# The weights' block sums made by adding DMA transfers: links set further apart, chains of different blocks between, and the third layer's sums moved to the second sweep

## The chip, the cores and the metric

One core of one Trainium2 chip runs the whole program. The metric is device microseconds (us) of that core for one execution.

## What is computed

The inputs are float32 and hold attention (4 batches, 12 heads, 448 tokens, 64 per head) and two pairs of feed-forward layers on the 1792 tokens (448 per batch, 768 wide). Cut to what matters:

```
q_n, k_n = rmsnorm(q, g_q), rmsnorm(k, g_k)
attn = softmax(q_n @ k_n.T / sqrt(64)) @ v
x = attn with heads side by side            # 1792 x 768
x = (sigmoid(x @ w_gate) * (x @ w_val)) @ w_out       # 768 -> 1536 -> 768
r = max(x @ w_in, 0); out = (r * r) @ w_out2          # 768 -> 2048 -> 768
```

## The kernel before, in words

The weights are worked through as 68 blocks of 128x768 numbers. Every product of a layer is made of three TensorE passes (high part by high part, high by low, low by high), so each block is split by ScalarE (`wsp<-wraw`, line 193, high part) and VectorE (line 194, low part) just before it is used. `w_load` (line 149) fetches a block on SyncE's DMA queue (SP) into one of three `wraw` buffers, and `w_ahead` keeps the loads and the splits a few blocks ahead of the use.

The program has four stages. A prologue does the attention of batch 0. `sweep(0)` takes batch 0 through all layers while the attention of batch 1 runs between its products; it also writes each converted block to DRAM (`w32`, line 182, on GpSimd's queue, POOL). `sweep(1)` takes batch 1 through all layers, in 204 steps, while the attention of batches 2 and 3 (twelve pairs of heads, some 16 or 17 steps each) runs between. Last, `joint` takes batches 2 and 3 through the layers together.

`joint` saves TensorE work by a scheme with seven products where eight blocks would be multiplied (`seven`). For it some operands are sums and differences of blocks of the weights. These are made in DRAM by DMA alone, and each such sum is two transfers of 192 KB: a copy on SP (line 596) and then an adding transfer on POOL (line 598, `accum_op=ALU.add`). A chain belongs to one pair of blocks and has three links, with two sums in the first and one in each of the others; a link reads what the link before it left in DRAM, so its copy waits until the adding transfer before has landed, and its adding transfer until its copy has landed. There are 12 chains for the first layer (`ws`, from `pair_chains`), 8 for the third (`wu`) and 8 for the last (`wt`, from `quad_chains`): 48, 32 and 32 sums.

Before, `add_up` issues all copies of a link on SP and at once all its adding transfers on POOL. `steps_of_1` puts the three links of chain p of the first layer at steps 12p+5, 12p+9 and 12p+13 of the second sweep. The third layer's chains are issued one link after the other in `joint`'s first layer (two links after each `seven`), and the last layer's in `joint`'s second layer (w_out, two links at each block) and after it.

Both queues run in order. SP also issues the weights' loads, the loads of q, k and v, and two transfers of the attention which move halves of `qs` and `ks` to other partitions (`a_dma`, lines 434 and 430); the scores of the next pair of heads (`att<-ks,qs`) wait for these. POOL also computes the power -0.5 of the rms norm (`ms<-ms,mhalf`, line 261), which VectorE needs for scaling q and k (line 265), which TensorE then transposes (`acc<-ident,qk`, line 571), and it spreads the softmax's reciprocals (`sb<-su`, line 320). In the second sweep and in `joint` TensorE's order is that of the program; the order on the other engines comes from a scheduler, which keeps every sum's transfers behind the last product issued before them (`held`), without a wait on the chip.

Of the kernel before, what the change touches and what calls it, by code (L numbers as in the profile page):

```python
# [12 lines left out]
ALU = mybir.AluOpType  # L13
# [4 lines left out]
def attention_moe_moe2_kernel(  # L18
# [541 lines left out]
    def held(i):  # L560
        tc.add_manual_dep(
            i.ins, latest[0].ins.name,
            mybir.DependencyInfo(mybir.DependencyClass.NoSync, mybir.DependencyReason.SCHED_ONLY), reason="order")
# [11 lines left out]
    def mm3(o, wb, kk, xh, xl, start, stop):  # L575
        wh, wl = wb[:, 0, kk], wb[:, 1, kk]
        mm(out=o, lhsT=wh, rhs=xh, start=start, stop=False)
        mm(out=o, lhsT=wh, rhs=xl, start=False, stop=False)
        mm(out=o, lhsT=wl, rhs=xh, start=False, stop=stop)
# [11 lines left out]
            halves.extend((wb[:, :, 0:3], wb[:, :, 3:6]))  # L591
        return halves.pop(0)

    def add_up(sums):
        for dst, first, second in sums:
            held(nc.sync.dma_start(out=dst, in_=first))
        for dst, first, second in sums:
            held(nc.gpsimd.dma_start(out=dst, in_=second, accum_op=ALU.add))  # L598

    def pair_chains(i0, i1, t):  # L600
        a11, a12, a21, a22 = (w32[i][:, h:h + 384] for i in (i0, i1) for h in (0, 384))
        s = [t[:, 384 * n:384 * (n + 1)] for n in range(4)]
        return [[(s[0], a21, a22), (s[2], a11, a21)], [(s[1], s[0], a11)], [(s[3], s[1], a12)]]
# [47 lines left out]
    def seven(parts):  # L651
        a, a2, b = (acc_tile()[:, :N] for _ in range(3))
        ps = att_tile()
        c, d = ps[:, 0, :N], ps[:, 1, :N]

        def product(o, name, start=True, stop=True):
            w = operand()
            for kk in range(3):
                mm3(o, w, kk, *parts[name, kk], start and kk == 0, stop and kk == 2)

        base = tmp("base")
        product(a, "B11")
        nc.scalar.copy(out=base, in_=a)
        product(a2, "B21")
        product(c, "T1")
        c11 = tmp("c11")
        nc.vector.tensor_tensor(out=c11, in0=a2, in1=base, op=ALU.add)
        yield 0, 0, c11, 1
        product(b, "T2")
        nc.vector.tensor_tensor(out=base, in0=base, in1=b, op=ALU.subtract)  # L670
        product(d, "T3")
        u = one.tile([128, 2, N], F32, tag="vs", name="u")
        nc.vector.tensor_tensor(
            out=u, in0=ps[:, :, :N], in1=base.unsqueeze(1).to_broadcast([128, 2, N]), op=ALU.add)
        c22 = tmp("c22")
        nc.vector.tensor_tensor(out=c22, in0=c, in1=u[:, 1], op=ALU.add)  # L676
        yield 1, 1, c22, -1
        last = att_tile()
        product(last[:, 1, :N], "T4")
        product(last[:, 0, :N], "B22")  # L680
        nc.vector.tensor_tensor(out=u, in0=last[:, :, :N], in1=u, op=ALU.add)
        yield 0, 1, u[:, 0], 1
        yield 1, 0, u[:, 1], -1

    def joint():
        edge = att_tile()
        for kc in range(NF + 1):
            n = 128 if kc < NF else TAIL
            nc.tensor.transpose(edge[:n, 0, kc * QR:(kc + 1) * QR], ident[:QR, :n], ident[:QR, :QR])
        later_sums = [c for kb in range(K4) for c in quad_chains(kb)]  # L690
        third_sums = [c for m in range(K2 // 2) for c in pair_chains(W3 + 2 * m, W3 + 2 * m + 1, w3s[m])]
        hr = one.tile([128, 27, N], F32R, tag="hr", name="h")
        rt = one.tile([128, 9, N], F32R, tag="rt", name="h")
        room = [hr[:, i] for i in range(27)] + [rt[:, i] for i in range(9)]
# [1 line left out]
        for g in range(K1 // 2):  # L696
            if g == 3:
                xy = one.tile([128, 12, N], F32R, tag="xy0", name="h")
                room += [xy[:, i] for i in range(12)]
            s = {}  # L700
            for i in range(2):
                q = two.tile([128, 2, N], F32, tag="qk", name="s")
                for n in range(2):
                    s[i, n] = q[:, n]
            for m, n, t, sign in seven(xp):
                e = s[m, n]
                nc.scalar.activation(out=e, in_=t, func=AF.Relu, scale=-1.0 * sign)
                nc.scalar.activation(out=t, in_=t, func=AF.Abs)
                nc.scalar.activation(out=e, in_=e, func=AF.Exp, scale=-1.0)
                nc.scalar.activation(out=t, in_=t, func=AF.Tanh, scale=0.5)  # L710
                nc.vector.scalar_tensor_tensor(out=e, in0=t, scalar=1.0, in1=e, op0=ALU.add, op1=ALU.mult)
            for c in (third_sums.pop(0) for _ in range(min(2, len(third_sums)))):
                add_up(c)
            for m, n, o, sign in seven(xp):
                e = s[m, n]
                if sign > 0:
                    nc.vector.tensor_tensor(out=e, in0=o, in1=e, op=ALU.mult)
                else:
                    nc.vector.scalar_tensor_tensor(
                        out=e, in0=o, scalar=-1.0, in1=e, op0=ALU.mult, op1=ALU.mult)  # L720
                hi, lo = room.pop(0), room.pop(0)
                h[2 * g + m, n] = hi, lo
                nc.scalar.copy(out=hi, in_=e)
                nc.vector.tensor_tensor(out=lo, in0=e, in1=hi.bitcast(F32), op=ALU.subtract)
            for c in (third_sums.pop(0) for _ in range(min(2, len(third_sums)))):
                add_up(c)
        order.extend(["raw64"] * 3 + ["qs", "xy1", "pt", "kq", "kq", "p", "p", "p"])
        yp = {}
        for j2 in range(3):
            y = {}  # L730
            for r in range(2):
                j = j2 + 3 * r
                q = two.tile([128, 2, N], F32, tag="qk", name="y")
                o = [acc_tile()[:, :N] for _ in range(2)]
                for b2 in range(2):
                    wb = block()
                    if later_sums or third_sums:
                        for _ in range(2):
                            if third_sums:
                                add_up(third_sums.pop(0))  # L740
                            elif later_sums:
                                add_up(later_sums.pop(0))
                    for kk in range(6):
                        k1 = 6 * b2 + kk
                        for n in range(2):
                            mm3(o[n], wb, kk, *h[k1, n], k1 == 0, k1 == K1 - 1)
                for n in range(2):
                    y[r, n] = q[:, n]
                    nc.scalar.activation(out=y[r, n], in_=o[n], func=AF.Copy, scale=0.5)
                split(yp, "B11" if r == 0 else "B21", j2, y[r, 0])  # L750
            split(yp, "B22", j2, y[1, 1])
            sums_of(yp, j2, y[0, 0], y[0, 1], y[1, 0], y[1, 1])
# [8 lines left out]
        for m2 in range(K2 // 2):  # L761
            for m, n, o, sign in seven(yp):
                k = 2 * m2 + m
                dst = r_of(k)[:, n * N:(n + 1) * N]
                nc.vector.scalar_tensor_tensor(
                    out=dst, in0=o, scalar=0.0, in1=o, op0=ALU.max if sign > 0 else ALU.min, op1=ALU.mult)
                if n == 1:
                    src = r_of(k)[:, 768:896]
                    nc.scalar.copy(out=plain[:, k, 0], in_=src)
                    nc.vector.tensor_tensor(  # L770
                        out=plain[:, k, 1], in0=src, in1=plain[:, k, 0].bitcast(F32), op=ALU.subtract)
            for _ in range(2):
                if later_sums:
                    add_up(later_sums.pop(0))
        for c in later_sums:
            add_up(c)
        yield
        row0 = 2 * N
        fsum = [rest[:, 768 * i:768 * (i + 1)].rearrange("p (k n) -> p k n", k=2) for i in range(3)] + [
# [508 lines left out]
    next(pro, None)  # L1288
    def steps_of_1():
        at = {}  # L1290
        for p in range(K1):
            for n, c in enumerate(pair_chains(4 * (p // 2) + p % 2, 4 * (p // 2) + 2 + p % 2, w1s[p])):
                at.setdefault(12 * p + 4 * n + 5, []).append((add_up, (c,)))
        order.extend(["xy1", "raw64", "raw64", "raw64", "kq", "qs", "kq", "p", "p", "pt", "p"])
        for j in range(3):
            for i, what in enumerate(("B11", "B21")):
                at.setdefault(158 + 6 * j + 3 * i, []).append((x_part, (j, what)))
        for i, what in enumerate(("sums", "B22")):
            at.setdefault(180 + 4 * i, []).append((x_part, (0, what)))
            at.setdefault(195 + 3 * i, []).append((x_part, (1, what)))  # L1300
        return at
# [63 lines left out]
```

## Time and profile before

| | us |
|---|---|
| median of 3 runs (1281.50, 1281.73, 1286.24) | 1281.73 |
| the profiled execution | 1287.66 |
| its span, first to last instruction | 1285.9 |
| TensorE busy in the span | 1243.1 (97%) |
| VectorE, ScalarE, GpSimd busy | 948.3, 792.0, 229.6 |
| chain of waits: TensorE 70%, DMA 15% of the span | |

The span is what the trace covers; the execution's own time has 1.8 us more around it. TensorE's busy time counts matmuls that run at a lower clock as busy too, so time is lost in idle pieces and in stretches with a lower granted clock.

### The profile page before, as it was taken

What the parts mean: (1) busy time and instruction counts of PE and PEld (TensorE: products, weight loads), DVE (VectorE), ACT (ScalarE), POOL (GpSimd) and SP (SyncE); (2) the same over time, 40 slices, a digit from 0 to 9 for tenths busy, and PEclk for the clock granted to TensorE, in tenths of its full rate; (3) what the DMA queues carried; (4) which work ended last, traced back from release to release, by engine and by line L of the source; (5) the groups of instructions that cost most, each with busy time, mean ns of one, the idle gap of its engine ahead of it and who ended that gap; (6) DMA issues with size and microseconds to landing.
All of it is one profiled execution on the core that took longest, in us unless ns stands there. A gap on an engine that the chain in (4) does not pass through costs nothing.

```text
span 1285.9 us, 19138 instructions
## 1 busy us (share of the span) xinstructions
PE 1243.1 (97%) x6599; PEld 1084.8 (84%) x6599; DVE 948.3 (74%) x1492; ACT 792.0 (62%) x1603; POOL 229.6 (18%) x236
## 2 busy tenths in 40 slices
PE   9999999999999989999999899999999996999998
PEld 6545788878879988888888899999999985999998
DVE  5866997878974878887878867888874324889873
ACT  5766887767865868776788765756672322235451
POOL 3311223212210322222222110011112221000000
PEclk8999999999999989999999999999999997999999
DMA  5445998888786776778777332577778777333443
GB/s 142 97 129 156 313 338 271 272 270 266 242 300 187 175 160 163 168 169 194 155 167 174 87 90 82 142 186 182 198 186 179 160 154 166 111 111 99 134 130 117
DMA packets 200545, 225.81 MB, mean 176 GB/s; under 512 B 83968, under 2 KB 178176, under 8 KB 200448
## 3 DMA queue, kind: packets, MB, share of 16 engines
q1 hardware_dynamic: 177024, 175.36, 47.0%
q0 software_dynamic: 21568, 48.77, 17.9%
q8 instruction: 52, 0.85, 0.3%
q10 hardware_dynamic: 1856, 0.46, 0.2%
q14 instruction: 45, 0.37, 0.1%
HBM read 185.99 MB, written 76.28 MB: 204 GB/s over the span
## 4 chain that ended last, share of the span: by engine, by line
PE 70%; DMA 15%; DVE 5%; ACT 4%; issue 3%; POOL 2%; SPq 1%; POOLq 0%; DVEq 0%; ACTq 0%
PE acc L566 41%; PE att L566 15%; DMA wt<-w 5%; DMA ws<-w 3%; PE att L291 3%; DMA ws<-ws 2%; PE att L571 2%; DMA wt<-wt 2%; POOL ms L261 2%; PE acc L345 2%; PE att L345 1%; PE acc L912 1%; PE acc L327 1%; DMA ks<-ks 1%; PE att L327 1%
## 5 line engine op out<-in xcount | busy, mean ns | idle before, releaser
L194 DVE TENSOR_TENSOR wsp<-wraw,wsp 128x768 fp32r<-128x768 f32 x246 | 236.4, 962 | 117.5 <-ACT wsp L193 115.4
L193 ACT CAST wsp<-wraw 128x768 fp32r<-128x768 f32 x246 | 205.6, 836 | 189.0 <-PE att L566 62.3
L566 PE MATMUL acc<-xy,wsp 128*128 128x448 f32 x1368 | 304.8, 373 | 6.2 <-ACT wsp L193 2.7
L566 PEld LDWEIGHTS acc<-xy,wsp 128*128 128x128 f32 x1368 | 252.5, 189 | 36.7 <-ACT wsp L193 5.0
L566 PE MATMUL att<-parts,wsp 128*128 128x448 f32 x720 | 156.2, 371 | 10.2 <-DVE c L676 6.6
L566 PEld LDWEIGHTS att<-parts,wsp 128*128 128x128 f32 x720 | 137.3, 191 | 22.4 <-issue 6.9
L566 PE MATMUL acc<-parts,wsp 128*128 128x448 f32 x540 | 118.1, 369 | 2.4 <-ACT parts L623 1.6
L566 PEld LDWEIGHTS acc<-parts,wsp 128*128 128x128 f32 x540 | 102.7, 190 | 11.2 <-ACT parts L623 2.0
L566 PE MATMUL acc<-wsp,rb 128*128 128x384 f32 x576 | 108.8, 338 | 0.0
L261 POOL TENSOR_TENSOR ms<-ms,mhalf 112x16 f32<-112x16 f32 (+1 forms) x25 | 84.8, 3395 | 95.0 <-DVE ms L260 95.0
L566 PEld LDWEIGHTS acc<-wsp,rb 128*128 128x128 f32 x576 | 99.5, 188 | 2.4 <-issue 1.3
L566 PE MATMUL acc<-hb,wsp 128*128 128x448 f32 x432 | 95.1, 371 | 0.0
L566 PE MATMUL acc<-h,wsp 128*128 128x448 f32 x432 | 87.7, 365 | 0.0
L566 PEld LDWEIGHTS acc<-hb,wsp 128*128 128x128 f32 x432 | 79.3, 188 | 9.1 <-issue 2.8
L566 PEld LDWEIGHTS acc<-h,wsp 128*128 128x128 f32 x432 | 81.2, 188 | 6.4
L598 POOL DMA_DIRECT2D ws<-w x48 | 40.0, 859 | 208.0 <-DMA ws<-ws 129.8
L167 ACT ACTIVATE wraw<-raw 128x768 f32<-128x768 f32 x64 | 58.4, 914 | 29.9 <-DVE wsp L194 15.2
L458 ACT ACTIVATE p<-att,nm 112x448 f32<-112x448 f32 x96 | 60.0, 631 | 20.8 <-DVE nm L447 19.9
L182 POOL DMA_DIRECT2D w<-wraw x64 | 35.3, 552 | 203.3 <-DVE wraw L175 191.6
L309 ACT ACTIVATE p<-att,nm 112x448 f32<-112x448 f32 x88 | 55.2, 637 | 21.9 <-DVE nm L297 19.9
L566 PE MATMUL acc<-wsp,rp 128*128 128x384 f32 x360 | 64.0, 334 | 0.0
L566 PEld LDWEIGHTS acc<-wsp,rp 128*128 128x128 f32 x360 | 62.6, 188 | 0.0
(205 smaller groups left out, 2035.9 us busy)
## 6 DMA issues: line engine op xcount, KB each, us to landing
wraw<-w SPq DMA_DIRECT2D x80, 384.0 KB, 3.6
w<-wraw POOLq DMA_DIRECT2D x64, 384.0 KB, 6.3
raw<-in_moe_w_out_dram SPq DMA_DIRECT2D x28, 768.0 KB, 7.1
wraw<-w SPq DMA_DIRECT2D x92, 192.0 KB, 2.6
raw<-in_moe_w_in_dram SPq DMA_DIRECT2D x16, 768.0 KB, 6.5
raw<-in_moe_w_gate_dram SPq DMA_DIRECT2D x12, 768.0 KB, 6.2
raw<-in_moe_w_val_dram SPq DMA_DIRECT2D x12, 768.0 KB, 6.5
ws<-w POOLq DMA_DIRECT2D x48, 192.0 KB, 4.4
```

The source lines that it names most:

```text
L167: size = nc.scalar.activation(out=t, in_=hi.bitcast(F32), func=AF.Prelu, scale=2.0 ** -112, alpha=2.0 ** 32)
L182: nc.gpsimd.dma_start(out=w32[i], in_=wraw[i])
L193: nc.scalar.copy(out=sp[:, 0], in_=t)
L194: nc.vector.tensor_tensor(out=sp[:, 1], in0=t, in1=sp[:, 0].bitcast(F32), op=ALU.subtract)
L261: nc.gpsimd.tensor_tensor(out=ms, in0=ms, in1=mhalf[:QR, 0:ms.shape[1]], op=ALU.pow)
L291: nc.tensor.matmul(out=ps[:QR, e, :S], lhsT=kq[a, 1, c * QR:(c + 1) * QR], rhs=kq[a, 0], start=True, stop=True)
L309: nc.scalar.activation(out=p[:, e], in_=ps[:QR, e, :S], func=AF.Exp, bias=nm[:, e:e + 1], scale=st["rq"][:, c, e:e + 1] if "rq" in st else ...
L327: nc.tensor.transpose(ps[:, kc, 0:QR], p[:, j * 128:(j + 1) * 128], ident[:QR, :QR])
L345: nc.tensor.matmul(out=o[e * D:(e + 1) * D], lhsT=v[:, kc, e], rhs=pt[:, (NF + 1) * e + kc if kc < NF else NF], start=(kc == 0), stop=(kc ...
L458: nc.scalar.activation(out=p[:, i * S:(i + 1) * S], in_=ps[:QR, i, :S], func=AF.Exp, bias=nm[:, i:i + 1], accum_out=su[:, c, e:e + 1])
L566: m = latest[0] = nc.tensor.matmul(**kw)
L598: held(nc.gpsimd.dma_start(out=dst, in_=second, accum_op=ALU.add))
```

## The change

`add_up` now issues either the copies of a link or its adding transfers. `set_out` gives each half its own place in a table: chain i of a list starts at `first + apart * i`, and its six halves lie `gap` apart. In the second sweep the places are steps (first 5, 8 apart, gap 8) and the list holds the 12 chains of the first layer and then the 8 of the third. For the last layer the places are beats, which `seven` counts by products and the w_out layer by two for each block (first 4, 14 apart, gap 10); what is left is issued at the end. Numbers and sizes of the transfers are as before.

```diff
-    def add_up(sums):
+    def add_up(sums, half):
         for dst, first, second in sums:
-            held(nc.sync.dma_start(out=dst, in_=first))
-        for dst, first, second in sums:
-            held(nc.gpsimd.dma_start(out=dst, in_=second, accum_op=ALU.add))
+            if half:
+                held(nc.gpsimd.dma_start(out=dst, in_=second, accum_op=ALU.add))
+            else:
+                held(nc.sync.dma_start(out=dst, in_=first))
+
+    def set_out(at, chains_, first, apart, gap):
+        for i, chain in enumerate(chains_):
+            for n, sums in enumerate(chain):
+                for half in range(2):
+                    at.setdefault(first + apart * i + gap * (2 * n + half), []).append((add_up, (sums, half)))
+
+    beat, at_beat = [0], {}
+
+    def beat_on(n=1):
+        for _ in range(n):
+            for fn, args in at_beat.pop(beat[0], []):
+                fn(*args)
+            beat[0] += 1
...
             for kk in range(3):
                 mm3(o, w, kk, *parts[name, kk], start and kk == 0, stop and kk == 2)
+            beat_on()
...
-        later_sums = [c for kb in range(K4) for c in quad_chains(kb)]
-        third_sums = [c for m in range(K2 // 2) for c in pair_chains(W3 + 2 * m, W3 + 2 * m + 1, w3s[m])]
+        set_out(at_beat, [quad_chains(kb) for kb in range(K4)], 4, 14, 10)
...
-            for c in (third_sums.pop(0) for _ in range(min(2, len(third_sums)))):
-                add_up(c)
...
-                    if later_sums or third_sums:
-                        for _ in range(2):
-                            if third_sums:
-                                add_up(third_sums.pop(0))
-                            elif later_sums:
-                                add_up(later_sums.pop(0))
+                    beat_on(2)
...
-            for _ in range(2):
-                if later_sums:
-                    add_up(later_sums.pop(0))
-        for c in later_sums:
-            add_up(c)
+        beat_on(30)
...
-        for p in range(K1):
-            for n, c in enumerate(pair_chains(4 * (p // 2) + p % 2, 4 * (p // 2) + 2 + p % 2, w1s[p])):
-                at.setdefault(12 * p + 4 * n + 5, []).append((add_up, (c,)))
+        set_out(at, [pair_chains(4 * (p // 2) + p % 2, 4 * (p // 2) + 2 + p % 2, w1s[p]) for p in range(K1)]
+                + [pair_chains(W3 + 2 * m, W3 + 2 * m + 1, w3s[m]) for m in range(K2 // 2)], 5, 8, 8)
```

The instructions move on two queues. On POOL, in the second sweep, the order before was this (the number after `ws_` is the chain):

```order
L598 DMA ws_181<-w_117 128x384 x2
L320 COPY sb<-su 112x512
L598 DMA ws_181<-w_115 128x384 x2
L261 TENSOR_TENSOR ms<-ms,mhalf 112x16
L598 DMA ws_182<-w_118 128x384 x2
L598 DMA ws_182<-w_116 128x384
L320 COPY sb<-su 112x512
L598 DMA ws_182<-w_116 128x384
```

and with the change it is this (line 597 is the adding transfer now):

```order
L597 DMA ws_180<-w_114 128x384 x2
L261 TENSOR_TENSOR ms<-ms,mhalf 112x16
L597 DMA ws_179<-w_111 128x384
L597 DMA ws_181<-w_117 128x384 x2
L320 COPY sb<-su 112x512
L597 DMA ws_180<-w_112 128x384
L597 DMA ws_182<-w_118 128x384 x2
L261 TENSOR_TENSOR ms<-ms,mhalf 112x16
```

Before, the adding transfers ahead of a power or a copy are links of one chain, each depending on the one ahead; now neighbours belong to different chains.

On SP, in the w_out layer of `joint`, the order before was this (`w_137` to `w_144` are loads of the layer's blocks):

```order
L149 DMA wraw<-w_143 128x768
L596 DMA wt_99<-wt_95 128x384
L596 DMA wt_95<-w_164 128x384
L596 DMA wt_103<-w_172 128x384
L596 DMA wt_107<-wt_99 128x384
L149 DMA wraw<-w_144 128x768
L596 DMA wt_99<-wt_95 128x384
L596 DMA wt_107<-wt_99 128x384
L149 DMA wraw<-w_139 128x768
```

and with the change it is this (line 599 is the copy):

```order
L149 DMA wraw<-w_141 128x768
L599 DMA wt_101<-wt_97 128x384
L149 DMA wraw<-w_142 128x768
L149 DMA wraw<-w_137 128x768
L149 DMA wraw<-w_138 128x768
L149 DMA wraw<-w_143 128x768
L599 DMA wt_108<-wt_100 128x384
L149 DMA wraw<-w_144 128x768
```

Before, up to four copies, some of them reading what the one ahead has just started, stood between two loads; now there are one or two, and four loads stand in a row.

## Rows read from the trace of the kernel before

**Rows 1.** The page: the span, and busy time of TensorE and of its weight loads.
```profile
span 1285.9 us, 19138 instructions
PE 1243.1 (97%) x6599; PEld 1084.8 (84%) x6599; DVE 948.3 (74%) x1492; ACT 792.0 (62%) x1603; POOL 229.6 (18%) x236
```

**Rows 2.** Busy time by stretch: stretch, length, engines, then TensorE's granted clock, DMA share, GB/s.
```profile
160.00:240.00 80.00, 80.00 (x422) 66.56 (x421) 68.24 (x101) 60.87 (x110) 21.35 (x23) 1.00 0.93 306
430.00:700.00 270.00, 257.00 (x1391) 230.51 (x1390) 217.88 (x362) 201.97 (x453) 68.69 (x60) 0.98 0.75 171
460.00:490.00 30.00, 27.42 (x138) 25.13 (x139) 22.19 (x35) 20.21 (x43) 7.00 (x7) 0.89 0.71 159
520.00:560.00 40.00, 37.16 (x199) 33.57 (x198) 32.28 (x54) 30.11 (x69) 12.79 (x9) 0.96 0.68 161
740.00:815.00 75.00, 73.92 (x450) 71.55 (x448) 54.68 (x89) 45.69 (x102) 4.92 (x3) 1.00 0.30 88
970.00:1050.00 80.00, 80.00 (x397) 74.15 (x396) 26.55 (x41) 21.96 (x38) 20.50 (x25) 1.00 0.77 167
1050.00:1095.00 45.00, 32.42 (x133) 28.06 (x132) 17.58 (x28) 10.84 (x19) 7.37 (x9) 0.85 0.68 156
```

**Rows 3.** TensorE in order of time, 1060 to 1090 us: start, length, [idle before <-releaser].
```profile
1061.25 0.47 PE L566 MATMUL acc<-parts,wsp 128*128 128x448 f32 x1 [1.58 <-ACT parts L623]
1062.53 1.03 PE L566 MATMUL acc<-parts,wsp 128*128 128x448 f32 x2 [0.80 <-DVE parts L624]
1068.74 0.47 PE L566 MATMUL att<-parts,wsp 128*128 128x448 f32 x1 [2.94 <-ACT parts L623]
1069.87 1.12 PE L566 MATMUL att<-parts,wsp 128*128 128x448 f32 x2 [0.66 <-DVE parts L624]
1089.45 3.70 PE L566 MATMUL att<-parts,wsp 128*128 128x448 f32 x9 [6.59 <-DVE c L676]
```

**Rows 4.** SP's queue and ScalarE in order of time, 1072 to 1086 us.
```profile
1072.00 9.17 SPq L596 DMA_DIRECT2D wt<-wt  x2
1081.26 1.01 SPq L149 DMA_DIRECT2D wraw<-wu  x2
1085.83 0.83 ACT L193 CAST wsp<-wraw 128x768 fp32r<-128x768 f32 x1 [9.83 <-DMA wraw<-wu]
```

**Rows 5.** Who waited for whom, whole span: TensorE's own, then SP's queue (us, times, longest).
```profile
PE acc L571 <- DVE qk L265: 8.4, 4, 3.3
SPq L596 <- DMA wt<-w: 77.2, 15, 8.6
```

**Rows 6.** The chain of waits around 455 to 463 us: start, length, what.
```profile
452.97 2.76 DMA ws<-ws
...
456.27 0.81 POOL ws L598
457.08 4.12 POOL ms L261
...
462.58 1.75 PE acc L571 x8
```

**Rows 7.** DMA queues, 430 to 700 us, then 970 to 1050: packets, MB, share.
```profile
q0 software_dynamic: 6336, 8.65, 24.3%
ws<-w POOLq DMA_DIRECT2D x44, 192.0 KB, 4.4
...
q1 hardware_dynamic: 5201, 8.66, 33.4%
```

**Rows 8.** DMAs from issue to landing: ks 430 to 705; ks 740 to 815; v in sweep 0; v 430 to 700.
```profile
DMA to landing us min/median/max: 2.8/5.0/8.2
DMA to landing us min/median/max: 3.0/3.0/3.0
DMA to landing us min/median/max: 6.1/6.4/7.5
DMA to landing us min/median/max: 2.0/2.9/4.3
```

**Rows 9.** Issue of ks on SP and TensorE's first product on it, a loose pair and the tightest.
```profile
467.68 0.64 SPq L430 DMA_DIRECT2D ks<-ks  x1
476.46 0.97 PE L566 MATMUL att<-ks,qs 128*112 128x448 f32 x4
663.34 0.93 SPq L430 DMA_DIRECT2D ks<-ks  x1
670.56 0.66 PE L566 MATMUL att<-ks,qs 128*112 128x448 f32 x2 [1.18 <-DMA ks<-ks]
```

More of the change, by code (lines that the diff above doesn't have):

```diff
@@ L724, in joint @@
                 nc.vector.tensor_tensor(out=lo, in0=e, in1=hi.bitcast(F32), op=ALU.subtract)
-            for c in (third_sums.pop(0) for _ in range(min(2, len(third_sums)))):
-                add_up(c)
         order.extend(["raw64"] * 3 + ["qs", "xy1", "pt", "kq", "kq", "p", "p", "p"])
@@ L771, in joint @@
                         out=plain[:, k, 1], in0=src, in1=plain[:, k, 0].bitcast(F32), op=ALU.subtract)
-            for _ in range(2):
-                if later_sums:
-                    add_up(later_sums.pop(0))
-        for c in later_sums:
-            add_up(c)
+        beat_on(30)
         yield
```

## The prediction

> **What bounds the kernel now.** I read the page first: TensorE is busy 1243.1 of 1285.9 us, so it is idle for only 43 us [rows 1]. No change of queues can win more than that, plus what is lost where its clock is lowered. So the next view is busy time by stretch, to see where the 43 us lie [rows 2]. Two places matter here. From 430 to 700 us, in the second sweep, TensorE is busy 257.0 of 270. From 1050 to 1095 us, at the end of the w_out layer of `joint` and the start of the third, it is busy 32.42 of 45, at a granted clock of 0.85. Between them, from 970 to 1050, it is busy all the time. Then I ask what each idle piece waits for.
>
> The late place: five pieces, 12.6 us together [rows 3]. The longest, 6.59 us, waits for VectorE's `c`, and behind it stands a weights' load: SP is held for 9.17 us by two copies of the last layer's chains, issues the load only at 1081.26, and ScalarE splits it at 1085.83 after 9.83 us of waiting [rows 4]. These copies wait because a link reads what the link before it has not finished; SP waits 77.2 us for such adding transfers in all [rows 5]. ScalarE works in order, so the 2.94 us piece, a split of layer parts, stood behind a late weights' load as well.
>
> The early place: TensorE waits four times, 8.4 us, for VectorE's scaled q and k before their transposes [rows 5]. The chain of waits shows why for one of them: a copy of a chain at 452.97, then the adding transfer on POOL at 456.27, then the power at 457.08, then the transposes at 462.58 [rows 6]. POOL stands at an adding transfer that waits for its copy, and the power is queued behind it.
>
> **The change part by part.** No sum, matmul or split is added or removed; 112 copies and 112 adding transfers remain. What changes is what stands between two links of a chain. In the second sweep eight steps lie between two halves. Six pairs of heads, 99 steps, lie between the two issues of `ks` at 467.68 and 663.34 [rows 9], so a step is 1.98 us; a copy is issued some 16 us before its adding transfer, and that 16 us before the next copy. Half a link lands in about 4.4 us [rows 7]. The waits of one queue for the other should therefore go.
>
> (a) Late place. The SP waits on `wt` go, loads come early, and the 6.59 and 2.94 us pieces go with them, also the 0.66 us that follows the second. What stays is the turn of the layer itself: the last block's result must be copied, subtracted and split before the third layer's products can go on, 1.58 and 0.80 us. I take 2.6 us left, so 10.0 us of idle time are won. The clock: 133 matmuls took 32.42 us, where 397 took 80.00 at full clock, 0.2015 each [rows 2]; 133 would take 26.8. So 5.6 us were lost to the clock, after the idle pieces; a piece of the length left has no such drop behind it elsewhere. Together **15.6 us**. The 32 `wu` sums leave `joint`, and the 32 `wt` sums take their room over a longer time, so its DMA load falls.
>
> (b) Early place. The four waits for q and k go, 8.4 us. Two of them had a lowered clock behind them: 0.89 over 30 us and 0.96 over 40 [rows 2] are 3.3 and 1.6 us. Together **13.3 us**. The rest of the idle time from 430 to 700 has other releasers, and I leave it.
>
> (c) The price: the second sweep now carries 80 sums instead of 48, and at its densest four sums in 8 steps where there were four in 12. On the adding queue 44 transfers took 24.3% of 270 us, 1.49 us of all 16 engines each [rows 7]. For a copy I take q1's time by bytes, 33.4% of 80 us for 8.66 MB, so 0.61 us for 192 KB. A sum costs 2.1 us, and 44 of them are 92 us of the 202 us (0.75 of 270) that the DMA engines were busy. One and a half times as many make 248 us, a share of 0.92. That is no overload, but transfers wait longer for each other, and the copies and adding transfers come four at a time.
>
> Who feels it? A weights' load is issued some two blocks of three steps (12 us) ahead of its split, and SP no longer waits for chains, so loads keep their cover. If it went, ScalarE would stop in order, as in (a). The transfers of `qs` and `ks` have the least room: from the issue of `ks` to the first product on it there are 8.8 us in a loose pair and 5.5 in the tightest, where TensorE already waits 1.18 us [rows 9]; landing takes 2.8 to 8.2 us, 5.0 in the middle [rows 8]. In the nine pairs from 430 to 705 us the spare time (room less landing, the same two views) is 3.3, 4.1, 3.2, 1.4, 0, 0, 2.2, 0 and 1.9 us.
>
> How much later will it land? The trace has no sweep with so many sums, so I bound it. Below: with no sums, at a share of 0.30, `ks` lands in 3.0 us, at 0.75 in 5.0 [rows 2, 8]; on that line 0.92 adds 0.8 us. It could even land earlier, since the pieces of a late SP are gone, so nothing is the lowest cost. Above: 96 KB transfers of `v` land in 2.9 us here and 6.4 in the first sweep, at a share of 0.93 [rows 2, 8], which adds 3.6. But there 768 KB loads are queued before them, here 192 KB copies, so I take the middle, 1.8. Then the pairs wait 1.8 three times and 0.4 once, **5.8 us**, too short for a lowered clock. The ends are 0, and for 3.6 us 16.8 of waiting (0.3, 0.4, 2.2, 3.6, 3.6, 1.4, 3.6, 1.7) and 7 more for the clock behind the three longest (2.4 each, the mean of the two above), so 24.
>
> (d) The loads of q and k, and the power on POOL with 4 x 0.81 us of issuing ahead of it at most, have five steps, 9.9 us, of room between the scaling and the transposes: nothing.
>
> **Sum**: 1287.66 (the profiled execution) - 15.6 - 13.3 + 5.8 = **1264.6**, I say 1265. The profiled execution is 5.9 us above the median, 1281.73; two of the three runs are near 1281.6 and one is at 1286.2, so the waits probably came out shorter in the fast ones. Then part of the 28.9 us is not there to be won, but then the result varies less too, and I leave 1265.
>
> The Trainium skill's "Perfetto Trace Analysis" (section "Identifying the Most-Contended Engine") holds that occupancy misleads for the 16 DMA engines and that bytes per time tell whether they bind. By rows the two differ here: a share of 0.92 is near the end, but 171 GB/s with 1.5 times the sums' bytes is about 204, where the first sweep moves 306 with TensorE never idle [rows 2]. By that rule (c) costs nothing; it is rival 1.
>
> **The rivals.**
>
> 1. *The added transfers cost nothing.* For: the GB/s just given. Against: `ks` lands later when sums run, 5.0 against 3.0 us [rows 8], and three pairs have no spare time. It gives 1287.66 - 28.9 = 1259.
>
> 2. *The gain is eaten in the second sweep.* `ks` lands 3.6 us later, the upper end, and (c) costs 24: 1287.66 - 28.9 + 24 = 1283, no change against the median. For: the measured `v` loads. Against: the shorter queue. The same time results if the late place keeps most of its idle time because the end of w_out, not the chains, holds the loads; the 9.17 us on SP [rows 4] speak against that.
>
> 3. *The bursts make it slower.* One beat puts four copies on SP just ahead of `qs` and `ks` in the later pairs, and four adding transfers on POOL beside them, 8.4 us of all engines at 2.1 a sum. If `ks` lands 5.5 us later, the nine pairs wait 2.2, 1.4, 2.3, 4.1, 5.5, 5.5, 3.3, 5.5 and 3.6, 33 us, and the six longest also lower the clock, 14 us: 1287.66 - 28.9 + 47 = 1306. It decides from about 4 us of delay on, where the cost passes 29 us. For: an 8.4 us burst can delay by that much whoever comes right behind it. Against: SP issues the copies behind a load that waits for a buffer, so mostly some us ahead of `qs`; and a stalled TensorE gives the transfers time.
>
> The skill's "DMA: Bandwidth & Descriptors" (section "Queues, rings and completion order") says that a transfer's completion is written only after all earlier writes of that DMA engine, on other queues too. By that rule `ks` would also wait for the adding transfers ahead of it, which is rival 3's mechanism. Landing times with and without sums agree in sign, no row shows the order itself.
>
> **How the numbers follow.** Forecast 0.50, rival 1 0.20, rival 2 0.17, rival 3 0.13. A difference of 0.5%, 6.4 us, is about what a measurement of this kernel can tell. Forecast and rival 1 lie below 1275: faster 0.70; rival 2 within: same 0.17; rival 3: slower 0.13. The range leaves out rival 3 and a little on the low side: 1254 (rival 1 less 5 for idle time of (b) that I left) to 1286 (rival 2 plus 3). The forecast's own range is 1258 to 1274.
>
> **What would show it.** Right: SP's waits for `wt<-w` and POOL's stand for `ws<-ws` gone; no wait of TensorE for q and k; one or two pieces of some 2.5 us at the turn to the third layer, with the clock at 1.00 behind; DMA share near 0.9 in the second sweep; `ks` landing in 6 to 7 us and a few waits for it. Wrong: a new long wait of TensorE for `ks`, or of ScalarE for a weights' load in the second sweep, or the late place's idle time unchanged.

## The result and the profile after

The changed kernel takes 1266.92 us in the median (1264.9 to 1268.89, 4 runs) against 1283.03 for the kernel before beside it: a ratio of 0.9871, 95% interval 0.9844 to 0.9898. In a later set of runs it was 1267.62 against 1286.25, 0.9855 (0.9822 to 0.9887). The forecast was 1265 in a range of 1254 to 1286. The profiled execution took 1264.9 us, 22.8 less than that of before; this overstates the gain, since it is the fastest of its four and that of before lies 4.6 us above its median. The medians differ by 16.1 and 18.6 us.

The page after: the span, and the engines' busy time. TensorE is idle for 28.5 us where it was 42.8 [rows 1], and its busy time, too, is 8.5 us shorter, for the same 6599 matmuls: that part goes with the clock.

```profile
span 1263.1 us, 19134 instructions
PE 1234.6 (98%) x6599; PEld 1079.7 (85%) x6599; DVE 946.4 (75%) x1492; ACT 791.9 (63%) x1603; POOL 228.6 (18%) x236
```

Busy time by stretch, the columns as in [rows 2]. Since 5 us were won before 530 us and more later, a stretch holds somewhat later work than before.

```profile
430.00:700.00 270.00, 262.07 (x1438) 234.63 (x1437) 223.99 (x377) 210.42 (x476) 87.65 (x85) 1.00 0.89 207
740.00:815.00 75.00, 71.71 (x429) 68.70 (x428) 55.30 (x91) 45.16 (x100) 9.98 (x9) 1.00 0.45 118
970.00:1050.00 80.00, 80.00 (x397) 74.15 (x396) 23.66 (x35) 21.08 (x36) 5.75 (x7) 1.00 0.36 87
1050.00:1095.00 45.00, 45.00 (x224) 41.61 (x223) 36.80 (x58) 17.03 (x30) 3.26 (x4) 1.00 0.52 132
```

From 1050 to 1095 us TensorE is now never idle, at full clock (it was 32.42 of 45 at 0.85). In the second sweep it is idle for 7.9 us of 270 (13.0 before), and the DMA share there rose from 0.75 to 0.89, near the 0.92 worked out. But from 740 to 815 it is idle for 3.3 us where it was 1.1.

Who waited for whom, the five of TensorE's that matter here (us, times, longest; lines left out are marked):

```profile
PE att L571 <- issue: 3.3, 1, 3.3
PE att L566 <- DMA qs<-qs: 3.3, 2, 2.0
...
PE att L566 <- DVE parts L639: 1.9, 1, 1.9
PE acc L571 <- DVE qk L265: 1.8, 1, 1.8
PE att L566 <- DMA ks<-ks: 1.7, 4, 0.7
```

The wait for scaled q and k fell from 8.4 to 1.8 us. The waits for `qs` and `ks` are new in this size: 5.0 together. Two more pieces grew: 3.3 us before the transposes of q and k at 717 us (2.3 before) and 1.9 us at 775 (none before). On SP no wait for an adding transfer is left; before it was 77.2 us for `wt` alone [rows 5]. POOL waited longest for the chains of the second sweep; these two lines are of the kernel before:

```profile
POOL ws L598 <- DMA ws<-ws: 129.8, 21, 12.7
...
POOL ws L598 <- DMA ws<-w: 56.8, 14, 20.2
```

Now POOL waits 0.8 us for copies of `ws`, and 24.0 us, three times, for copies of `wu`. It still waits long for copies of `wt`, in `joint`, where it has nothing but sums to do.

TensorE issues the same matmuls in the same order in both kernels, so one can be laid over the other. The table is worked out from the two traces: when the same matmul starts, and by how much the changed kernel is ahead.

```
matmul no.   before us   after us   ahead us
      2415       462.6      460.5        2.1   transposes of q and k
      2435       468.6      463.8        4.8
      2764       532.6      523.8        8.8
      3616       694.6      681.9       12.6
      3665       703.9      694.4        9.5   first products on ks
      3806       731.9      724.9        7.0
      4091       780.1      775.7        4.4
      5510      1061.3     1055.2        6.1   turn to the third layer
      5585      1092.9     1070.4       22.5
```

So the second sweep wins 12.6 us up to matmul 3616 (682 us in the changed kernel), then gives 8.2 back until 776; the turn to the third layer wins 18.1.

### The profile page after: what moved, and what is told of

Its sections match the earlier page's. It is cut to its first block, busy times and chain, and to the rows that moved or that the text cites. A ratio compares the mean times of both kernels' runs of the same rounds, so it can differ in the third digit from the quotient of the medians.

```text
span 1263.1 us, 19134 instructions
## 1 busy us (share of the span) xinstructions
PE 1234.6 (98%) x6599; PEld 1079.7 (85%) x6599; DVE 946.4 (75%) x1492; ACT 791.9 (63%) x1603; POOL 228.6 (18%) x236
## 4 chain that ended last, share of the span: by engine, by line
PE 86%; DVE 4%; ACT 3%; DMA 3%; issue 2%; SPq 1%; POOL 0%; DVEq 0%; ACTq 0%; POOLq 0%
PE acc L566 54%; PE att L566 17%; PE att L291 3%; PE att L571 3%; DMA ks<-ks 2%; PE acc L345 2%; PE att L345 1%; PE acc L914 1%; PE acc L327 1%; PE att L327 1%; PE acc L571 1%; DVE wsp L194 1%; ACT p L458 1%; DMA out_dram<-ob 0%; ACT wsp L193 0%
## 5 line engine op out<-in xcount | busy, mean ns | idle before, releaser
L566 PE MATMUL att<-parts,wsp 128*128 128x448 f32 x720 | 152.4, 365 | 0.0
L261 POOL TENSOR_TENSOR ms<-ms,mhalf 112x16 f32<-112x16 f32 (+1 forms) x25 | 81.8, 3273 | 186.6 <-DVE ms L260 174.5
L597 POOL DMA_DIRECT2D wt<-w x32 | 26.2, 860 | 288.8 <-DMA wt<-wt 208.3
L458 ACT ACTIVATE p<-att,nm 112x448 f32<-112x448 f32 x96 | 60.0, 631 | 16.1 <-DVE nm L447 15.0
```

What stands on the lines that cost most here:

```text
L261: nc.gpsimd.tensor_tensor(out=ms, in0=ms, in1=mhalf[:QR, 0:ms.shape[1]], op=ALU.pow)
L458: nc.scalar.activation(out=p[:, i * S:(i + 1) * S], in_=ps[:QR, i, :S], func=AF.Exp, bias=nm[:, i:i + 1], accum_out=su[:, c, e:e + 1])
L566: m = latest[0] = nc.tensor.matmul(**kw)
```

## The experiments

Two theories of the gain stood against each other. The first: setting the links apart frees SP and POOL, and moving the third layer's sums costs something. The second: `joint` got well because 32 of its sums left it. For the price in the sweep there were three: bursts right ahead of `ks`, or the total load, or VectorE's order.

**Only the late place.** The second sweep issues a link's halves together, as before; in `joint` both the third and the last layer's sums are set out.

```diff
-        set_out(at, [... 12 chains of the first layer ...] + [... 8 of the third ...], 5, 8, 8)
+        for p, chain in enumerate([... 12 chains of the first layer ...]):
+            for n, sums in enumerate(chain):
+                at.setdefault(12 * p + 4 * n + 5, []).extend([(add_up, (sums, 0)), (add_up, (sums, 1))])
-        set_out(at_beat, [quad_chains(kb) for kb in range(K4)], 4, 14, 10)
+        set_out(at_beat, [... 8 chains of the third ...], 2, 8, 8)
+        set_out(at_beat, [quad_chains(kb) for kb in range(K4)], 52, 12, 8)
```

> Second sweep as before the change (12 chains, a link's copies and adding transfers together), both the third and the last layer's sums stay in the joint stage but with their halves 8 beats apart. Theory 1 (the spacing of the links frees SP in the joint stage): the idle time at the turn to the third layer is under 1 us instead of 12.6, its lowered clock is gone, the waits for scaled q and k in the second sweep stay at about 8 us; the time is 14 to 18 us under the kernel before, 1265 to 1269. Theory 2 (it was the 32 sums leaving the joint stage that freed it): most of the loss stays, 1278 to 1283.

Measured: 1266.77 us (1262.03 to 1274.78), 0.9846 (0.9789 to 0.9903) of before. Its stretches:

```profile
430.00:700.00 270.00, 258.04 (x1421) 231.42 (x1420) 221.74 (x371) 207.21 (x469) 69.52 (x62) 1.00 0.75 173
1050.00:1095.00 45.00, 45.00 (x224) 41.59 (x223) 38.75 (x60) 16.80 (x30) 6.60 (x8) 1.00 0.71 176
```

The turn is free of waits with all 64 sums still in `joint`. The spacing did it, not the move; the second theory falls. The sweep is as it was, with 7.1 us of waiting for scaled q and k. Against the 1285.56 beside it the late place is worth 18.8 us (12 to 27 by the interval; laid over matmul by matmul, the turn wins 18.2).

**All spaced, nothing moved.** As above, and the second sweep's 12 chains are set out as well, 12 steps apart.

```diff
-        set_out(at, [... 12 chains of the first layer ...] + [... 8 of the third ...], 5, 8, 8)
+        set_out(at, [... 12 chains of the first layer ...], 5, 12, 8)
```

> All links spaced, but the third layer's sums stay in the joint stage: second sweep with 12 chains 12 steps apart and 8 steps between halves, joint stage with 8 chains 8 beats apart and 8 chains 12 beats apart. Theory 1: the gain of the late place stays whole, TensorE's waits for ks and qs fall from 4.8 to under 2 us, the two losses after 715 us (3.3 us before transposes of q and k, 1.9 us before the products of P and v) get smaller; 1257 to 1262, below the changed kernel's 1267. Theory 2: the late place comes back with the 32 sums, 1275 or more.

Measured: 1254.97 us (1253.44 to 1257.17), 0.9744 (0.9692 to 0.9795): better than both kernels, by more than expected.

```profile
430.00:700.00 270.00, 266.88 (x1472) 240.58 (x1470) 229.08 (x387) 216.13 (x487) 66.41 (x60) 1.00 0.76 177
815.00:970.00 155.00, 155.00 (x767) 143.63 (x766) 117.81 (x167) 94.70 (x167) 32.79 (x40) 1.00 0.83 205
```

TensorE is idle for 3.1 us of these 270; no wait for `qs` or `ks` is among its first eleven. And `joint` carries the third layer's sums, at a DMA share of 0.83, without any idle time. The step from the run before, 1266.77 to 1254.97, is what spacing gives in the sweep: 11.8 us, uncertain by several, since the four runs there lie between 1262 and 1275. Laid over the kernel before, this version is 14.2 us ahead at matmul 3616, still 14.0 at 4091, and 32.0 at 5585: it gives nothing back after 694 us, and the turn wins the same 18.

**Moved, not spaced.** 20 chains in the second sweep, a link's halves together, and the last layer's sums as before the change.

```diff
-        set_out(at, [... 12 chains of the first layer ...] + [... 8 of the third ...], 5, 8, 8)
+        for p, chain in enumerate([... all 20 ...]):
+            for n, sums in enumerate(chain):
+                at.setdefault(9 * p + 3 * n + 5, []).extend([(add_up, (sums, 0)), (add_up, (sums, 1))])
-                    beat_on(2)
+                    for _ in range(2):
+                        if later_sums:
+                            both = later_sums.pop(0)
+                            add_up(both, 0)
+                            add_up(both, 1)
```

> Third layer's sums moved to the second sweep as in the change, but no spacing: 20 chains 9 steps apart, links 3 steps apart, a link's copies and adding transfers together; last layer's sums two links at each block of the w_out layer as before. Theory 1: SP still waits for wt transfers in the joint stage and the turn to the third layer still loses 5 us or more; in the second sweep POOL still stands at its transfers, and the waits for scaled q and k are 8 us or more: 1278 to 1300. Theory 2: like the changed kernel, 1265 to 1270.

Measured: 1323.85 us (1321.27 to 1326.33), 1.0282 (1.0235 to 1.033), worse than I gave it. TensorE's waits, then SP's:

```profile
PE acc L571 <- DVE qk L265: 24.3, 8, 7.0
PE att L566 <- DMA ks<-ks: 8.1, 4, 3.6
PE att L566 <- DVE c L692: 6.2, 1, 6.2
```

```profile
SPq L599 <- DMA ws<-w: 116.3, 23, 7.8
SPq L599 <- DMA wu<-w: 86.5, 16, 8.3
SPq L599 <- DMA wt<-w: 81.4, 16, 8.7
```

The early wait grows from 8.4 to 24.3 us, with more sums in the sweep and with links 3 steps apart where they were 4. The long wait at the turn (6.2 us, 6.59 before [rows 3]) is there, although the third layer's sums are out of `joint`; of the 12.6 us of idle time there 9.4 are left. The last layer's chains alone stop SP long enough.

**No sums in the second sweep.** The changed kernel without these sums; the loads that would read a sum read an unsummed block, so it computes something else.

```diff
-            ops += [(r0, 0), (r0, 384), (t, 0), (t, 384), (t, 768), (r1, 384), (t, 1152)]
+            ops += [(r0, 0), (r0, 384), (r0, 0), (r0, 384), (r0, 0), (r1, 384), (r0, 384)]
-        set_out(at, [... 12 chains of the first layer ...] + [... 8 of the third ...], 5, 8, 8)
```

> The changed kernel without the 80 sums of the second sweep: the first and third layers of the joint stage load an unsummed block where they would load a sum, so the outputs are others; the last layer's sums stay. It measures the price of the sums in the sweep. Theory 1: TensorE's waits for ks and qs (4.8 us) go, so do 1.9 us at 775 and 1 to 3 us at 717: 1254 to 1259. Rival (the sums cost nothing there, the waits after 715 have another cause): 1263 to 1267.

Measured: 1254.58 us (1253.7 to 1256.08). From 430 to 700 us TensorE's busy time is the same as with 48 spaced sums, at a DMA share of 0.44:

```profile
430.00:700.00 270.00, 266.82 (x1474) 240.65 (x1473) 229.59 (x386) 215.21 (x484) 30.53 (x17) 1.00 0.44 113
```

So the change's 80 sums in the sweep cost some 12 us, and 48 well spaced ones cost nothing that can be measured.

**Four steps earlier.** The changed kernel with its bursts in another place against `ks`.

```diff
-                + [pair_chains(W3 + 2 * m, W3 + 2 * m + 1, w3s[m]) for m in range(K2 // 2)], 5, 8, 8)
+                + [pair_chains(W3 + 2 * m, W3 + 2 * m + 1, w3s[m]) for m in range(K2 // 2)], 1, 8, 8)
```

> The changed kernel with the 20 chains of the second sweep four steps earlier (first step 1 instead of 5), so that a beat's four copies and four adding transfers lie 2 to 6 steps before the issue of qs and ks in the pairs from 500 us on, instead of 0 to 3. All else, the number of sums too, as in the change; VectorE's scaling of q and k for the last pair but one is back ahead of the splits of x in its order. If the bursts right ahead of ks make it late: its waits fall from 4.8 to under 2 us. If it is the total load: they stay at 4 to 6. If VectorE's order made the stop at 717 us: 3.3 us become 2.3 and the slow matmuls behind it (2.4 us) go. Together 1258 to 1262 by bursts and order, 1262 to 1264 by order alone, 1266 to 1268 by neither.

Measured: 1267.77 us (1265.86 to 1268.64), in the range given for "neither", though both things expected came true. The first product on `ks` waits 0.08 us in one pair only. `ks` lands as follows in the changed kernel and in this one (430 to 705 us; 5.0 in the middle before [rows 8]):

```profile
DMA to landing us min/median/max: 3.2/5.8/7.5
```

```profile
DMA to landing us min/median/max: 3.7/4.9/6.0
```

At the same DMA share, 0.89, the middle is that of before. The stop at 717 us shrinks to 2.3 us, and the matmuls behind it run at full clock. But a new wait took its place:

```profile
PE acc L571 <- DVE qk L265: 8.6, 5, 2.2
```

One of the five is the 1.8 us of the other versions; three more are of 2.1 to 2.2 us, and behind two of these (at 495 and 562 us) the granted clock is 0.83 over the next 10 us. It is not POOL this time. VectorE's order explains it: for these pairs the scheduler now puts the scaling (L265) behind the split of the softmax parts (L487, L491). The chain before one of these waits, at 495 us, where the power had ended at 488.4, runs through VectorE alone:

```profile
492.71 0.77 DVE parts L487
493.49 0.27 DVE parts L491
493.77 0.28 DVE parts L491
494.05 0.03 issue
494.08 1.30 DVE qk L265 x2
```

**Six steps between halves.** The changed kernel with the last 8 of `set_out(at, ..., 5, 8, 8)` made 6.

> The changed kernel with 6 steps instead of 8 between the halves in the second sweep: copies and adding transfers never fall on the same step, and at most three on one; 6 steps are 12 us, more than the landing of a half. Bursts: waits for qs and ks fall to 1 to 3 us, and the order on VectorE is again that of before the change, so 1258 to 1263. Load alone: waits as in the change, 1262 to 1264 by the order.

Measured: 1262.2 us (1259.34 to 1267.04), 0.9838 (0.9791 to 0.9886). The time fits the forecast of "load alone" plus order, but the waits do not: `ks` lands later than in the change, and TensorE waits more for it.

```profile
PE att L566 <- DMA ks<-ks: 6.4, 4, 2.2
```

```profile
DMA to landing us min/median/max: 2.8/6.3/9.9
```

The gain is after 715 us: at matmul 3806 it has caught up with the change, 0.1 us ahead, and at 4091 it is 2.6 ahead. Here the scaling before 717 us stands ahead of the splits on VectorE again. So the landing of `ks` changes with where the sums fall, but smaller bursts were no cure.

**As dense, but not moved.** As all spaced, nothing moved, with the 12 chains 8 steps apart instead of 12.

> As the version with all sums spaced and the third layer's in the joint stage, but the second sweep's 12 chains 8 steps apart instead of 12, so that they are as dense as in the change from step 45 to step 93, and are over by step 133. If density makes ks late: 2 to 4 us of waits up to some 660 us, nothing lost after 700 us, 1256 to 1260. If only the mere number of sums or the tail costs: as the version 12 apart, 1254 to 1256.

Measured: 1257.26 us (1256.53 to 1257.51), 0.9795 (0.9753 to 0.9837), some 2 us above the version 12 apart. The waits for `qs` and `ks` are back, 3.3 us, all by 600 us, and none falls after the chains are over:

```profile
PE att L566 <- DMA qs<-qs: 2.5, 1, 2.5
...
PE att L566 <- DMA ks<-ks: 0.8, 2, 0.5
```

**Two steps between halves.** As all spaced, nothing moved, with gap 2 in place of 8 in all three lists.

> As the version with all sums spaced and the third layer's in the joint stage (12 apart, gap 8), but only 2 steps or beats between halves: 4 us, just about one landing. If the links' distance against the landing time is what frees the queues, POOL and SP wait again for some halves: 1262 to 1278, part of the loss for scaled q and k back, and 0 to 6 us at the turn to the third layer. If setting other chains between (or issuing the halves apart at all) is enough: 1254 to 1258.

Measured: 1285.8 us (1281.28 to 1295.89, 10 runs), 1.0009 (0.9975 to 1.0042): no faster than the kernel before, more loss than I expected. SP waits for `ws` as before the change and for `wu` more (66.2 us before), for `wt` less. The largest loss is in a new place, `joint`'s first layer:

```profile
SPq L599 <- DMA wu<-w: 90.2, 16, 7.1
SPq L599 <- DMA ws<-w: 60.9, 17, 7.8
SPq L599 <- DMA wt<-w: 29.9, 10, 6.8
```

```profile
815.00:975.00 160.00, 145.17 (x680) 131.45 (x679) 106.89 (x150) 83.41 (x147) 32.26 (x40) 0.96 0.78 185
```

TensorE's waits in this stretch are all for VectorE's `c`, and the chain of waits there runs through late loads of the weights:

```profile
PE att L566 <- DVE c L692: 14.8, 6, 4.7
```

Laid over the kernel before, the version is 8.5 us ahead at matmul 4091, 14.0 behind at 5300, and 4.2 ahead at 5585. So the turn keeps its whole 18 us, the sweep a part of its gain, and 22.5 us are lost between, in the first layer. A beat is nine matmuls there (1.8 us), so two are less than a landing; in the w_out layer it is eighteen, and two are 7.3 us. Issuing the halves apart by less than a landing is not enough. This run does not separate distance from order: with 2 steps between halves the neighbours on a queue are again mostly links of one chain.

**The two versions side by side.** The changed kernel and the one with all spaced and nothing moved, once more, on one chip.

> The changed kernel again, on the same chip as the next one: 1263 to 1269.

> The version with all sums spaced and the third layer's left in the joint stage, again, beside the changed kernel: 1253 to 1258, 9 to 13 us under it. If the two came within 4 us here, the earlier difference would have been one of chips.

Measured: 1267.62 (1262.32 to 1270.19, 0.9855, 0.9822 to 0.9887) and 1254.58 (1252.54 to 1256.09, 0.9754, 0.9725 to 0.9783). The difference of 13.0 us stands. It arises in the sweep: laid over the kernel before, the changed kernel is 1.1 us ahead at matmul 4091 in this execution and the other 13.8, and from there to the end each wins 18.4. So the last layer's different places do not matter.

## Why the prediction was right, and where its terms were not

**The mechanism** of both places held. Chains stop SP and POOL when a link waits for the link before; set apart, they don't (SP 77.2 us for `wt` and none, POOL 186.6 us for `ws` and 0.8). The first three runs show this against the rival that the move did it. That other chains stand between the links came with the distance in every run, so what it does by itself is not shown.

**(a)** was 15.6 us and measured 18.1 in the trace, 18.8 between medians. The clock part was right. I had kept 2.6 us of idle time for the turn itself, and none is left: that wait was not the turn's own. [Rows 3] name ScalarE and VectorE as releasers of those pieces. But the trace of the kernel before shows ScalarE standing at a late weights' load right there too; the copy of the last result, and its split behind the 1.58 us, come after it in ScalarE's order:

```profile
1059.04 0.83 ACT L193 CAST wsp<-wraw 128x768 fp32r<-128x768 f32 x1 [10.52 <-DMA wraw<-w]
```

With loads in time ScalarE and VectorE split while TensorE works through 18 matmuls that don't need the last result. The changed kernel, without idle time:

```profile
1052.15 3.81 PE L566 MATMUL acc<-parts,wsp 128*128 128x448 f32 x18
```

I read a releaser's name as a cause and did not ask what had held that releaser.

**(b)** was 13.3 us and measured 11.8 between medians, 14.0 in the trace at matmul 4091; within the noise it was right. 1.8 us of the wait for scaled q and k stayed in every version with its links set apart, also without sums, where VectorE's own order makes it; it was never POOL's.

**(c)** was 5.8 us and measured 12 to 13 between medians (9.6 and 12.7 at matmul 4091 in the two pairs of traces, with and without the move), the one term that was badly sized. The step "who feels it?" named the first products on `qs` and `ks`, and these did wait 5.0 us in the profiled execution (`ks` landing 0.8 us later in the middle, at the lower end of the bounds). That this is near 5.8 is luck in part: only 1.7 of it is for `ks`, which the working followed, and 3.3 for `qs`, which it named and did not follow. The tightest pair's room of 5.5 us was also misread: it is counted to a product at 668.81 that started before `ks` had landed; to the product in [rows 9] it is 6.0. That such waits are too short for a lowered clock did not hold in the second profiled execution: behind 2.4 us of waiting for `qs` the granted clock was 0.83 from 695 to 705 us.

What it missed lies after 700 us, in a stretch that the working treated as untouched. It costs some 5 us in both profiled executions of the changed kernel:

- The stop before the transposes of q and k at 717 us grew from 2.3 to 3.3 us. Before, the scaling (L265) stood ahead of the splits of x (L624, now L639) and of the softmax parts on VectorE; now it stands behind both, with the power done at 711.16. Why the scheduler chose so no run shows. The granted clock behind the stop is the larger part of the cost.

VectorE before, then in the changed kernel, in order of time, then the changed kernel's stretches of 10 us around the stop:

```profile
722.30 1.28 DVE L265 TENSOR_TENSOR qk<-qk,ms 112x512 f32<-112x512 f32 x2
723.50 1.69 DVE L624 TENSOR_TENSOR parts<-xwhole,parts 128x448 fp32r<-128x448 f32 x3
```

```profile
712.92 1.68 DVE L639 TENSOR_TENSOR parts<-xwhole,parts 128x448 fp32r<-128x448 f32 x3
714.53 0.85 DVE L487 TENSOR_TENSOR parts<-att,parts 128x672 fp32r<-128x672 f32 x1
715.39 0.56 DVE L491 TENSOR_TENSOR parts<-att,parts 64x112 fp32r<-64x112 f32 x2
715.98 1.29 DVE L265 TENSOR_TENSOR qk<-qk,ms 112x512 f32<-112x512 f32 x2
```

```profile
705.00:715.00 10.00, 9.09 (x57) 8.53 (x55) 8.89 (x16) 9.26 (x22) 5.46 (x4) 1.00 0.69 164
717.00:727.00 10.00, 9.63 (x42) 9.35 (x43) 6.01 (x11) 3.58 (x6) 0.00 (x0) 0.69 0.39 95
```

Of the 1.00 ahead of the stop 0.69 is left behind it, and the sequence of matmuls fell back by 2.4 us there. In the version four steps earlier, where the order is the old one and the stop 2.3 us, it is 1.00 behind. The working looked at the orders on POOL and SP and not at VectorE's.

- At 775 us TensorE waits for VectorE, which had waited for a buffer whose result had not yet gone out. The transfer of the result, 2.2 us to landing in the middle in the kernel before, takes 6.30 here, right behind two adding transfers on POOL. First POOL's line, then the chain of waits:

```profile
763.92 1.66 POOL L597 DMA_DIRECT2D wu<-w  x2
```

```profile
765.39 6.30 DMA out_dram<-ob
...
771.72 0.04 DVE t L653
```

Without sums in the tail the 1.9 us are gone (no sums in the sweep; as dense, but not moved). That it was the adding transfers and not SP's order the version with six steps shows: SP issues the same transfers at the same times (764.97 and 765.40), no adding transfer stands beside them on POOL until 769.27, they land in 1.9 and 2.0 us, and the wait is gone.

**The sum** came out within 3 us of the medians, but by errors that partly cancel: the gain of (a) was 3 us too small, the price of (c) 6 to 7 too small. The base was too high as well: larger sets of runs of the kernel before have medians of 1283.03 to 1286.25, so the 1281.73 of three runs was low and the profiled execution lies 1.4 to 4.6 us above, not 5.9. That the number came so close is luck.

**The rivals.** Rival 1, that the added transfers cost nothing, fails: the versions without the move, or without the sums, are 12 us faster. At 207 GB/s, far from the 306 of the first sweep, transfers with little room landed late. The Trainium skill's "Perfetto Trace Analysis" (section "Identifying the Most-Contended Engine") would have bytes per time decide. For loads with a buffer ahead that agrees with the runs (`joint` at 205 GB/s and a share of 0.83 has no idle time), for a wait on a single landing it does not help. For rival 3's mechanism, a burst right ahead of `ks`, speaks that four steps earlier the delay goes; against it, that six steps between halves have smaller bursts and a later landing. In any case it is small: 1 us in the middle, not 4. Whether `ks` waits for adding transfers on the other queue no run separates. That it would is what the Trainium skill's "DMA: Bandwidth & Descriptors" (section "Queues, rings and completion order") says.

## What to carry to other kernels

When two in-order queues hand a chain of transfers back and forth, issue the halves well over one landing apart (12 to 16 us in the sweep here, where a half lands in 4 to 7; at some 4 us both queues waited again) and let the queues' other work stand between. Leave such work spread over the stages instead of gathering it where transfers with a hard deadline run: the same spacing without the move is 12 to 13 us faster. And where a scheduler sets the order, look at the order on every engine: a scaling that moved behind six splits cost 2.4 us, most of it by the clock.

## What the runs showed of the hardware that I had not expected

- At one DMA share, 0.89, and with the same transfers, `ks` landed in 5.8, 4.9 and 6.3 us in the middle (7.5, 6.0 and 9.9 at most) in the change, four steps earlier, and with gap 6. So the share alone does not fix it; what does was not separated.
- After a stop of 3.29 us TensorE's granted clock was 0.69 over the next 10 us, a mean between its two levels (1.2 and 2.4 GHz), and after one of 2.3 us at the same place it stayed at 1.00, the full 2.4 GHz. The length of the stop alone does not tell: stops of 2.08 and 2.19 us (four steps earlier) and of 2.41 (the changed kernel again) had 0.83 behind them, and in the latter one of 2.91 us had 1.00.
- An output transfer of 192 KB landed in 6.30 us behind two adding transfers on the other queue, and in 2.0 us, issued at the same time, without them.
- A DMA share of 0.83 over 155 us, with weights' loads on the same queue, left TensorE without any idle time.
